# Seven products for the scores of the first two key tiles of a chunk, and three orders in a two-batch conformer block on one core

## The chip, the core and the metric

The kernel runs on one core of a Trainium2 chip. The metric is the device time of one execution in microseconds. The core has a matrix engine (PE, with its weight loads PEld beside it), a vector engine (DVE), an activation engine (ACT), a slow general engine (POOL), and a queue (SP) that issues nearly all DMA transfers. Each engine runs its own instructions strictly in the order in which they were written, and waits on semaphores of the others.

## The reference

One conformer block on x of 2 batches by 4000 tokens by 512 features, in bfloat16. Feed-forward 1 has a hidden width of 2048; attention has a single head of width 512; a convolution module with a batch norm and a second feed-forward follow.

```python
h = _layernorm(x); h = _silu(h @ w_ff1_a) @ w_ff1_b
x1 = x + 0.5 * h
h = _layernorm(x1); q, k, v = h @ w_q, h @ w_k, h @ w_v
scores = jnp.einsum('btd,bsd->bts', q, k) * scale
attn = jnp.einsum('bts,bsd->btd', _softmax(scores), v) @ w_o
x2 = x1 + attn
...
h = _layernorm(x3); h = _silu(h @ w_ff2_a) @ w_ff2_b
return _layernorm(x3 + 0.5 * h)
```

## The kernel before

**Tiling.** The tokens of both batches are cut into NCK = 16 chunks, eight to a batch: seven of 512 tokens and one of 416. The first feed-forward runs over all chunks, then attention over the query chunks g = 0 to 15 with 32 steps kt (one per 128 keys) in each, then the end of the convolution, then the second feed-forward over all chunks. The convolution of chunk g - 2 and the layer norm of chunk g - 1 run inside the attention steps of chunk g.

**Products.** Nearly all large products use a form of Strassen's method with seven products for a 2 by 2 block instead of eight. `score_quad` (L2096) does so for the scores of four key tiles at a time. Its left factors are parts of the transposed keys `hT` and three sums of them (`KF`, made by `k_sums`, L2069, once per batch and stored to DRAM as `kfd`, then loaded again for each later chunk by `k_stream`, L2091). Its right factors are parts of the transposed queries `qT` and four differences of them (`QF`). Four of its steps are spread over four values of kt, in PSUM banks 0 (c), 1 (x) and 2 (h). A step of the quad is: a few matmuls into a bank, then a copy by ACT or an addition by DVE, in PSUM, on which the next matmuls into that bank wait.

**The first two key tiles.** Of the 32 key tiles, 28 go into the seven quads (tiles 2 to 29). Tiles 0, 1 and 30 are computed plainly in `scores` (L1791): four matmuls of 512 columns each, into bank 0 for kt = 0 and bank 1 for kt = 1, and `exp_pair` (L1901) takes the exponential. At the same steps, `query_quad` (L1849) makes the transposed queries of the next chunk, in the same banks 0, 1 and 2: step 0 at kt = 31, steps 1 and 2 at kt = 0, step 3 at kt = 1.

**What else PE has at the start of a chunk.** `late_first`, `late_second` and `late_third` (L2229 to L2257) finish the product of probabilities and values of the chunk before, at kt = 0 to 6, in other banks; `conv_quad` (L2553) runs at kt = 2 to 7. The values of the new chunk begin at kt = 7.

**What sets the order.** The program text gives an order only within a tick. All operations are first collected in `Plan` (L112), with an assumed duration for each. A list schedule is made from these when the kernel is built: for PE among the operations within 8 us of PE time of the first one still open (`front` gives the products of a score quad 1 us of priority), for the other engines and the DMA queue among what is ready, the most urgent first. The emitted order on each engine is that of the plan; at run time nothing is reordered. An operation given to `either` may go to ACT or DVE, as the plan finds it better. `after(n, f)` puts f into the program n ticks later.

**The head.** `head` (L1237) makes the layer norm of the first four token tiles with `ln_tiles` (L1206, lag 1): on DVE the statistics (`ln_stats`), the mean and variance (`ln_mean`), then on POOL the power -0.5 (`ln_factor`), then the normalised tile on DVE, PE transposes, and blocks of the first product. `wa_sums` (L1409) makes four sums of the weights on DVE for the quads of chunk 1.

**The second feed-forward's second chunk.** Its layer norm is an `ln_job` (L1170) with all four tiles' statistics first, one POOL power for all, one `ln_shift`, four normalisations on ACT (`eng="ACT"`), and four DMA transposes on the SP queue. Its input tiles 2 and 3 are finished by `pw2_residual` only in chunk 0's steps f (their products stand at f = 2 and f = 4 of sixteen). `ff_weights` (L1321) makes sums of the second weight matrix on DVE, at the steps in `second.plan`.

Every recorded operation has the line L95 in the profile, that of the call object that issues it; groups are told apart by the names of the tiles.

Of the kernel before, what the change touches and what calls it, by code (L numbers as in the profile page):

```python
# [5 lines left out]
F32 = mybir.dt.float32  # L6
# [9 lines left out]
TILE = 128  # L16
# [543 lines left out]
class Conformer:  # L560
# [35 lines left out]
    def memory(self):  # L596
# [120 lines left out]
        self.hq = A.view(2048, QUADS * 2048).rearrange("p (q u r e j k) -> p q u r e j k", q=QUADS, u=2, r=2, e=2, j=2)  # L717
        self.kfd = nc.dram_tensor("kfd", [B, QUADS, 128, 1536], BF16, kind="Internal").ap()
        self.b_kfd = [[Buf("kfd") for _ in range(QUADS)] for _ in range(B)]
        self.vhd = nc.dram_tensor("vhd", [PAIRS, 128, 2 * D], BF16, kind="Internal").ap()  # L720
# [69 lines left out]
        self.thl = [W.view(24576 + s * 1024, CHUNK) for s in range(4)]  # L790
        self.b_thl = [W.buf("thl", 24576 + s * 1024, 2 * CHUNK) for s in range(4)]
        self.b_th = [W.buf("th", 24576 + s * 2048, 4 * CHUNK) for s in range(2)]
        homes = ((24576, 26624), (8192, 10240))
# [376 lines left out]
    def ln_job(self, c, kind, eng="DVE", plan=(1, 1, 2, 2, 3, 4, 5, 5, 6, 6), slot=None, pe=None):  # L1170
# [32 lines left out]
        for ti in range(n):  # L1203
            self.after(norm[ti], lambda ti=ti: tile(ti))

    def ln_tiles(self, c, sl, prepare=None, engs=("ACT", "ACT", "ACT", "DVE"), src=None, lag=2):  # L1206

# [11 lines left out]
        for ti in range(TPC):  # L1219
            if prepare:  # L1220
                prepare(ti)
            if ti and lag > 1:
                self.ln_mean(sl, ti - 1)
            self.ln_stats(c, sl, ti, src)
            if ti and lag > 1:
                self.ln_factor(sl, ti - 1)
            if ti >= lag:
                finish(ti - lag)
                yield ti - lag
            if lag == 1 or ti == TPC - 1:  # L1230
                self.ln_mean(sl, ti)
                self.ln_factor(sl, ti)
# [175 lines left out]

    def wa_sums(self, w, b_w, n, part):  # L1409

# [8 lines left out]
        for h in range(2):  # L1419
            self.S.op("DVE", lambda e, h=h: e.tensor_tensor(out=out[:, h], in0=x[:, h], in1=y[:, h], op=op),  # L1420
                      reads=more + rd, writes=wr)

# [646 lines left out]
    def k_sums(self, g, q, step):  # L2069

        S, n, b = self.S, (QUADS * g + q) % 2, g // TCB
        x = self.hq[:, q]
        b_x = [self.b_hT[kt // TPC][kt % TPC] for kt in self.quad_tiles(q)]
        if step == 4:
            self.store(self.kfd[b][q], self.KF[n].rearrange("p m u j k -> p (m u j k)"), self.b_KF[n], [self.b_kfd[b][q]])
            return
        a11, a12, a21, a22 = [x[:, :, r, e].rearrange("p u j k -> p u (j k)") for r in range(2) for e in range(2)]
        s1, s2, s4 = [self.KF[n][:, m].rearrange("p u j k -> p u (j k)") for m in range(3)]
# [3 lines left out]
        S.op("DVE", lambda e: e.tensor_tensor(out=out, in0=u, in1=v, op=op), reads=rd + b_x, writes=wr)  # L2082

    def k_here(self, g, q, half):
# [6 lines left out]
    def k_stream(self, g, q):  # L2091
        n, b = (QUADS * g + q) % 2, g // TCB
        self.load(self.KF[n].rearrange("p m u j k -> p (m u j k)"), self.kfd[b][q], self.b_KF[n],
                  reads=[self.b_kfd[b][q]])

    def score_quad(self, g, q, step):  # L2096
# [5 lines left out]
        b_t = [self.b_hT[kt // TPC][kt % TPC] for kt in self.quad_tiles(q)]  # L2102
        n = (QUADS * g + q) % 2
        part = lambda r, e: (lambda u, j: tiles[:, u, r, e, j], lambda u: b_t[2 * u + r])
# [97 lines left out]
    def forms(self, g, kt):  # L2202
# [637 lines left out]
    def program(self, any_score):  # L2840
# [50 lines left out]
        def ff1(c):  # L2891
            def hook(f):
# [261 lines left out]
        def ff2(c):  # L3154
            def hook(f):
# [106 lines left out]
```

## Time and profile before

| what | value |
|---|---|
| device time, median of 3 runs | 1855.84 us (1855.61 to 1857.74) |
| device time of the profiled execution | 1854.86 us |
| span of the profiled execution, first to last instruction | 1850.7 us |
| attention, one middle chunk (from one start to the next) | 61.6 us |
| DMA traffic | 228.51 MB, 123 GB/s on average |

The span is cut into the stages by the names of the tiles: the first feed-forward up to about 385 us, attention to about 1370 us, the end of the convolution to about 1403 us, the second feed-forward after that. Names on the left of an arrow are written, those on the right are read; `s` and `y` are PSUM banks 0 to 3 and 4 to 7, `sums`, `xt`, `keys`, `work` and `wff` are regions of SBUF that hold many things. A matmul's mean duration counts its way through the array, which overlaps the next one: the step from the start of one to the start of the next is what counts. Some matmul records are missing: a group of "x3" or "x7" with a gap of one matmul ahead of it had four or eight.

### The profile page before, as it was taken

To read this page: it belongs to the slowest core of one execution; us is meant where nothing else is said; L and a number is where in the kernel's file an instruction comes from. 1 tells how busy PE (TensorE), PEld (TensorE's weight loads), DVE (VectorE), ACT (ScalarE), POOL (GpSimd) and SP (SyncE) were. 2 spreads that over 40 slices of the span, in tenths; PEclk is the share of its full clock that TensorE was granted. 3 is DMA by queue.
4 is the path that set the end of the run, shared out by engine and by line. 5 is a ranking of instruction groups with operands and counts; after the bars stand their busy time and mean duration, and the time that the engine had idled before them with its cause. 6 is when DMAs were issued, how large, how long until landed. Compare 5 with 4: busy or idle time off the path is not lost.

```text
span 1850.7 us, 40576 instructions
## 1 busy us (share of the span) xinstructions
PE 1827.9 (99%) x15992; PEld 1512.7 (82%) x16090; DVE 1477.2 (80%) x3200; ACT 1358.0 (73%) x2412; POOL 145.8 (8%) x356
## 2 busy tenths in 40 slices
PE   9999999999999999999999999999999999999998
PEld 6888888866888888888778888888875888888887
DVE  8889998868766777677876777777778988888896
ACT  6887777755656877678776876787768778778776
POOL 3000000000000000000000000000010000000000
PEclk9999999999999999999999999999999999999999
DMA  8233344287645655457944434443466222221211
GB/s 202 84 91 85 83 113 98 70 240 231 183 130 142 180 161 152 119 142 175 244 136 130 129 108 115 137 125 104 125 213 171 56 70 72 66 58 48 61 35 56
DMA packets 312521, 228.51 MB, mean 123 GB/s; under 512 B 191154, under 2 KB 283125, under 8 KB 312068
## 3 DMA queue, kind: packets, MB, share of 16 engines
q1 hardware_dynamic: 311796, 225.59, 44.3%
q8 instruction: 128, 2.10, 0.5%
q14 instruction: 69, 0.57, 0.1%
q10 hardware_dynamic: 528, 0.26, 0.0%
HBM read 128.99 MB, written 55.82 MB: 100 GB/s over the span
## 4 chain that ended last, share of the span: by engine, by line
PE 92%; DVE 3%; DMA 2%; ACT 1%; issue 1%; SPq 0%; POOL 0%; DVEq 0%; ACTq 0%
PE y L95 48%; PE s L95 44%; DVE work L95 1%; DMA work<-work 1%; DVE sums L95 1%; ACT work L95 1%; DVE wff L95 0%; DVE xt L95 0%; DMA dcvd<-wff 0%; DVE s L95 0%; DVE keys L95 0%; ACT sums L95 0%; ACT keys L95 0%; DMA work<-lrowd 0%; DMA xt<-in_x_dram 0%
## 5 line engine op out<-in xcount | busy, mean ns | idle before, releaser
L95 ACT ACTIVATE sums<-s 128x512 bf16<-128x512 f32 (+4 forms) x498 | 291.4, 586 | 134.4 <-PE s L95 131.1
L95 ACT ACTIVATE keys<-s 128x512 bf16<-128x512 f32 (+3 forms) x275 | 157.1, 575 | 134.2 <-PE s L95 110.4
L95 DVE TENSOR_TENSOR sums<-sums 128x512 bf16<-128x512 bf16 (+3 forms) x528 | 202.1, 399 | 64.5 <-ACT sums L95 52.7
L95 PE MATMUL y<-work,keys 128*128 128x256 bf16 x1920 | 244.4, 273 | 0.6 <-DVE work L95 0.6
L95 PE MATMUL s<-sums 128*128 128x256 bf16 (+1 forms) x1428 | 212.5, 272 | 0.6 <-DVE s L95 0.3
L95 PE MATMUL y<-wff,keys 128*128 128x256 bf16 (+2 forms) x1590 | 208.9, 276 | 0.2
L95 ACT ACTIVATE work<-xt,work 128x512 bf16<-128x512 bf16 x264 | 202.6, 786 | 7.4 <-DVE work L95 5.6
L95 PEld LDWEIGHTS y<-work,keys 128*128 128x128 bf16 x1920 | 187.6, 98 | 23.6 <-DVE work L95 1.2
L95 PE MATMUL y<-sums,keys 128*128 128x256 bf16 (+1 forms) x1440 | 206.5, 270 | 0.0
L95 PE MATMUL s<-work,keys 128*128 128x256 bf16 (+4 forms) x1370 | 197.0, 282 | 2.3 <-DVE xt L95 0.6
L95 PE MATMUL y<-work,wff 128*128 128x256 bf16 (+3 forms) x1324 | 197.3, 272 | 1.0 <-ACT keys L95 0.8
L95 DVE TENSOR_TENSOR keys<-keys 128x1024 bf16<-128x1024 bf16 (+2 forms) x262 | 170.5, 665 | 22.3 <-ACT keys L95 17.9
L95 PEld LDWEIGHTS y<-wff,keys 128*128 128x128 bf16 (+1 forms) x1592 | 151.2, 98 | 30.2 <-issue 3.3
L95 DVE BATCH_NORM_STATS2 work<-xt 128x6 f32<-128x512 bf16 x251 | 163.2, 682 | 2.4 <-DMA xt<-in_x_dram 1.7
L95 PEld LDWEIGHTS s<-sums 128*128 128x128 bf16 x1428 | 138.9, 98 | 23.2 <-DVE s L95 0.6
L95 PEld LDWEIGHTS y<-sums,keys 128*128 128x128 bf16 x1440 | 138.1, 98 | 21.6 <-issue 3.3
L95 POOL TENSOR_TENSOR work<-work 128x4 f32<-128x4 f32 (+3 forms) x107 | 91.6, 858 | 766.7 <-DVE work L95 754.3
L95 PEld LDWEIGHTS s<-work,keys 128*128 128x128 bf16 (+1 forms) x1400 | 113.1, 97 | 43.4 <-ACT sums L95 2.2
L95 PEld LDWEIGHTS y<-work,wff 128*128 128x128 bf16 x1324 | 127.3, 98 | 18.8 <-issue 1.5
L95 PE MATMUL y<-sums,xt 128*128 128x256 bf16 (+1 forms) x960 | 140.9, 270 | 0.3 <-DVE sums L95 0.3
L95 PE MATMUL s<-xt,keys 128*128 128x256 bf16 (+1 forms) x872 | 132.6, 270 | 1.9 <-DVE s L95 1.6
L95 DVE TENSOR_TENSOR s<-s,xt 128x512 f32<-128x512 f32 (+1 forms) x119 | 81.5, 685 | 63.0 <-PE s L95 53.3
(162 smaller groups left out, 3345.1 us busy)
## 6 DMA issues: line engine op xcount, KB each, us to landing
xt<-kfd SPq DMA_DIRECT2D x98, 384.0 KB, 3.2
xt<-v12d SPq DMA_DIRECT2D x105, 256.0 KB, 3.1
xd<-xt SPq DMA_DIRECT2D x28, 512.0 KB
xt<-xd SPq DMA_DIRECT2D x28, 512.0 KB, 4.0
out_dram<-xt SPq DMA_DIRECT2D x14, 512.0 KB, 2.9
xt<-in_x_dram SPq DMA_DIRECT2D x13, 512.0 KB, 4.3
dcvd<-wff SPq DMA_DIRECT2D x48, 128.0 KB
keys<-dcvd SPq DMA_DIRECT2D x12, 512.0 KB, 3.9
```

The costliest lines, as they stand in the source:

```text
L95: return getattr(eng, self.name)(*self.args, **self.kw)
```

## The change

The scores of key tiles 0 and 1 are computed together by seven products of a half quad, `half_quad`, in the 13 chunks 2 to 7 and 9 to 15. Chunks 0, 1 and 8 keep the plain form. The sums of keys for it (`KF[0]`, half a quad's size) are made in chunks 1 and 8, stored, and loaded for chunks 3 to 7 and 10 to 15; the two homes of `KF` are numbered anew, so that in chunks other than 0 and 8 quad 0's sums lie in home 1; quad 0's load moves from kt = 25 to kt = 29 and quad 1's from kt = 29 to kt = 1 of its own chunk.

In the head, the statistics of a tile come after the mean of the tile before, and the first of `wa_sums` after the fourth normalised tile. The layer norm of the second feed-forward's chunk 1 is made in two halves (`ln_halves`), its normalisations on either engine. One `ff_weights` moves from f = 15 to f = 13.

```diff
+    def ln_halves(self, c, plan):
+        S, sl, s = self.S, self.nxt("ln", self.LN_SLOTS), c % 2
+        def factors(two):
+            for ti in range(two.start, two.stop):
+                self.ln_mean(sl, ti)
+            S.op("POOL", lambda e: e.tensor_tensor(out=self.rs[sl][:, two], in0=self.mv[sl][:, two, 1],
+                                                   in1=self.neghalf[0:TILE, two], op=ALU.pow),
...
+        def tile(ti):
+            self.ln_norm(c, sl, ti, self.ltm[ti][0:TILE, :], self.b_ltm[ti], "any")
+            self.transpose(self.lnT[s][:, ti], self.ltm[ti], [self.b_ltm[ti]], [self.b_lnT[s][ti]])
+        for k, at in enumerate(plan):
+            two = slice(2 * k, 2 * k + 2)
+            for n in range(2):
+                self.after(at[n], lambda ti=2 * k + n: self.ln_stats(c, sl, ti))
+            self.after(at[2], lambda two=two: factors(two))
+            self.after(at[3], lambda two=two: shift(two))
+            for n in range(2):
+                self.after(at[4 + n], lambda ti=2 * k + n: tile(ti))
...
-            self.ln_stats(c, sl, ti, src)
+            self.ln_stats(c, sl, ti, src, [self.b_mv[sl][ti - 1]] if ti and lag == 1 else ())
...
+    @staticmethod
+    def k_home(g, q):
+        return (q + (g % TCB > 0)) % 2 if q >= 0 else 0
...
+    def half_quad(self, g, step):
+        S, s, hw = self.S, g % TCB % 2, width(g) // 2
+        (cx, b_cx), (hy, b_hy) = self.bank(0), self.bank(2)
+        c, x = cx[:, 0:hw], cx[:, hw:2 * hw]
+        h, y = hy[:, 0:hw], hy[:, hw:2 * hw]
+        m5, b_m5 = self.m5h[:, 0:hw], self.b_m5h
...
+        def product(k, out, b_ps, start=False):
+            (a, b_a), (m, b_m) = forms[k]
+            for j in range(2):
+                self.mm(out, a(j), m(j), start and j == 0, j == 1, [b_a, b_m(j)], b_ps, skip_group_check=True)
+        def plus(out, b_out):
+            S.op("DVE", lambda e: e.tensor_tensor(out=out, in0=h, in1=m5, op=ALU.add), reads=[b_hy, b_m5], writes=[b_out])
+        if step == 0:
+            product(1, c, b_cx, True)
+            product(5, x, b_cx)
+            self.act(m5, x, AF.Copy, [b_cx], [b_m5])
+        elif step == 1:
+            self.act(h, c, AF.Copy, [b_cx], [b_hy])
+            product(6, h, b_hy)
+            product(2, c, b_cx)
+            plus(x, b_cx)
+        elif step == 2:
+            product(7, h, b_hy)
+            plus(y, b_hy)
+            product(3, x, b_cx)
+            self.exp_pair(g, 0, cx, b_cx)
+        else:
+            product(4, h, b_hy)
+            self.exp_pair(g, 1, hy, b_hy)
...
-                if plain and kt < KT - 1 or kt < 2 or kt == KT - 2:
+                if plain and kt < KT - 1 or g % TCB < 1 + (g < TCB) and kt < 2 or kt == KT - 2:
...
                     S.front(1000)
-                    self.score_quad(g, *divmod(kt - 2, 4))
+                    for step in ((0,), (1, 2), (3,))[kt] if kt < 3 and g % TCB > (g < TCB) else ():
+                        self.half_quad(g, step)
+                    if kt > 1:
+                        self.score_quad(g, *divmod(kt - 2, 4))
                     S.front(0)
...
+        for at in {1: (26, 27), TCB: (29, 30)}.get(g, ()):
+            if kt == at:
+                self.k_here(g, -1, kt % 2 == g % TCB)
...
-        if r == 0 and 1 < q and (g % TCB if q < QUADS else g and (g + 1) % TCB):
-            self.k_stream(g + q // QUADS, q % QUADS)
-        if g == 0 and kt == 30 or g == 1 and kt == 1:
-            self.k_stream(1, kt % 2)
+        if r == 0 and q and (g % TCB if q < QUADS else g and (g + 1) % TCB) and (q != QUADS or g % TCB > (g < TCB)):
+            self.k_stream(*((g, q) if q < QUADS else (g + 1, q - QUADS - 1)))
+        if g == 0 and kt == 30:
+            self.k_stream(1, 0)
...
-        second.plan = {(0, 12): (0,), (0, 15): (1,), (1, 0): (2,), (1, 8): (3,)}
+        second.plan = {(0, 12): (0,), (0, 13): (1,), (1, 0): (2,), (1, 8): (3,)}
...
-                    self.wa_sums(self.Wa, self.b_Wa, (0, 1, 3, 2)[f % 4], (f - 8) // 4)
+                    self.wa_sums(self.Wa, self.b_Wa, (0, 1, 3, 2)[f % 4], (f - 8) // 4, self.b_ltm[3:] if f == 8 else ())
...
-                        self.ln_job(1, "in", "ACT", (3, 4, 5, 7, 7, 8, 8, 8, 9, 9))
+                        self.ln_halves(1, ((2, 2, 3, 4, 5, 5), (5, 6, 7, 8, 8, 9)))
```

In the half quad, banks 0 and 2 hold two halves each: c and x (tile 0 for the two halves of the queries) in bank 0, h and y (tile 1) in bank 2. Every copy and addition in a bank excludes matmuls into the other half of that bank, since the bank is one buffer to the synchronisation.

More of the change, by code (lines that the diff above doesn't have):

```diff
@@ L717, in memory @@
         self.hq = A.view(2048, QUADS * 2048).rearrange("p (q u r e j k) -> p q u r e j k", q=QUADS, u=2, r=2, e=2, j=2)
-        self.kfd = nc.dram_tensor("kfd", [B, QUADS, 128, 1536], BF16, kind="Internal").ap()
-        self.b_kfd = [[Buf("kfd") for _ in range(QUADS)] for _ in range(B)]
+        self.hh = A.view(0, 1024).rearrange("p (r e n) -> p r e n", r=2, e=2)
+        self.kfd = nc.dram_tensor("kfd", [B, QUADS + 1, 128, 1536], BF16, kind="Internal").ap()
+        self.b_kfd = [[Buf("kfd") for _ in range(QUADS + 1)] for _ in range(B)]
         self.vhd = nc.dram_tensor("vhd", [PAIRS, 128, 2 * D], BF16, kind="Internal").ap()
@@ L1407, in ff_second, with wa_sums @@
                 f == 0, f == FC - 1, [self.b_Wb[f], b_p], b_ps, inc=inc)
-    def wa_sums(self, w, b_w, n, part):
+    def wa_sums(self, w, b_w, n, part, behind=()):
         at = slice(part * HF // 2, (part + 1) * HF // 2)
@@ L1420, in wa_sums @@
             self.S.op("DVE", lambda e, h=h: e.tensor_tensor(out=out[:, h], in0=x[:, h], in1=y[:, h], op=op),
-                      reads=more + rd, writes=wr)
+                      reads=more + rd + list(behind), writes=wr)
     def wa_ahead(self, w, step):
@@ L2082, in k_sums, with k_move @@
         S.op("DVE", lambda e: e.tensor_tensor(out=out, in0=u, in1=v, op=op), reads=rd + b_x, writes=wr)
+    @staticmethod
+    def k_home(g, q):
+        return (q + (g % TCB > 0)) % 2 if q >= 0 else 0
+    def k_move(self, g, q, away):
+        n, b = self.k_home(g, q), g // TCB
+        here, there = self.KF[n].rearrange("p m u j k -> p m (u j k)"), self.kfd[b][q % (QUADS + 1)].rearrange("p (m x) -> p m x", m=3)
+        if q < 0:
+            here, there = here[:, :, 0:HD], there[:, :, 0:HD]
+        if away:
+            self.store(there, here, self.b_KF[n], [self.b_kfd[b][q]])
+        else:
+            self.load(here, there, self.b_KF[n], reads=[self.b_kfd[b][q]])
     def k_here(self, g, q, half):
@@ L2102, in score_quad @@
         b_t = [self.b_hT[kt // TPC][kt % TPC] for kt in self.quad_tiles(q)]
-        n = (QUADS * g + q) % 2
+        n = self.k_home(g, q)
         part = lambda r, e: (lambda u, j: tiles[:, u, r, e, j], lambda u: b_t[2 * u + r])
```

33 lines of the change are left out of this document (24 added, 9 removed).

## The prediction

> **What bounds the kernel now.** I read the page first, then the busy time by windows, then the timeline of single engines at the three places that the change touches.
>
> ```profile
> span 1850.7 us, 40576 instructions
> PE 1827.9 (99%) x15992; PEld 1512.7 (82%) x16090; DVE 1477.2 (80%) x3200; ACT 1358.0 (73%) x2412; POOL 145.8 (8%) x356
> ...
> PE 92%; DVE 3%; DMA 2%; ACT 1%; issue 1%; SPq 0%; POOL 0%; DVEq 0%; ACTq 0%
> ```
>
> PE is busy for 1827.9 of 1850.7 us and is 92% of the chain that ends last. So a matmul taken away is worth its step in the stream, unless a wait takes the place; and only 22.8 us of PE's time are idle at all. The windows say where.
>
> ```profile
> 0.00:25.00 25.00, 22.25 (x167) 12.60 (x168) 20.87 (x63) 13.97 (x25) 5.70 (x17) 1.00 1.03 257
> ...
> 633.38:695.00 61.62, 61.40 (x548) 51.37 (x551) 47.05 (x109) 46.50 (x86) 4.14 (x16) 1.00 0.53 158
> ...
> 1400.00:1425.00 25.00, 21.85 (x155) 13.97 (x156) 21.18 (x47) 23.24 (x40) 2.41 (x3) 1.00 0.71 199
> 1425.00:1450.00 25.00, 24.44 (x205) 20.00 (x207) 23.25 (x42) 20.31 (x34) 1.01 (x1) 1.00 0.21 55
> 1450.00:1475.00 25.00, 24.36 (x209) 20.32 (x210) 22.44 (x46) 16.69 (x28) 1.01 (x1) 1.00 0.22 59
> ```
>
> The columns are the window, its length, then PE, PEld, DVE, ACT and POOL busy. A middle chunk of attention has 0.2 us of idle PE in 61.6, while DVE (47) and ACT (46.5) have room. The head has 2.75 us of idle PE, and the first 75 us of the second feed-forward 3.15 + 0.56 + 0.64 = 4.35 us. These are the change's three places: matmul time in attention, idle time at the other two.
>
> **The half quad: what it saves.** PE's timeline at the start of chunk 5 (start, duration, operation, count), and a piece of the chain of waits that is PE alone:
>
> ```profile
> 699.72 1.03 PE L95 MATMUL s<-work,keys 128*128 128x512 bf16 x4
> 700.58 0.60 PE L95 MATMUL s<-work,sums 128*128 128x256 bf16 x4
> ...
> 706.02 0.60 PE L95 MATMUL s<-xt 128*128 128x256 bf16 x4
> ...
> 715.19 0.60 PE L95 MATMUL s<-xt 128*128 128x256 bf16 x4
> ...
> 77.28 1.75 PE y L95 x16
> ```
>
> Four matmuls of 512 columns take 700.58 - 699.72 = 0.86 us, 0.215 each; sixteen of 256 take 1.75, 0.1094 each. Removed per chunk: 8 x 0.215 = 1.72 us. Added: 7 products of 2 matmuls, 14 x 0.1094 = 1.53. That saves 0.19 us in eleven chunks of 512 tokens, 2.1 us; in the two of 416 about 13/16 of it, 0.3 together. Sum **2.4 us**.
>
> [...]
>
> **What it adds elsewhere.** Per chunk two copies by ACT and two additions by DVE, 256 wide, in PSUM; no such width from PSUM stands in the trace, so I take the line through the two widths that do.
>
> ```profile
> L95 ACT ACTIVATE xt<-s 128x512 f32<-128x512 f32 x103 | 61.3, 595 | 33.0 <-PE s L95 32.3
> L95 ACT ACTIVATE xt<-s 128x416 f32<-128x416 f32 x16 | 8.2, 513 | 6.0 <-PE s L95 6.0
> L95 DVE TENSOR_TENSOR s<-s,xt 128x512 f32<-128x512 f32 x103 | 71.9, 698 | 52.2 <-PE s L95 46.8 <-ACT xt L95 4.0
> L95 DVE TENSOR_TENSOR s<-s,xt 128x416 f32<-128x416 f32 x16 | 9.6, 601 | 10.8 <-PE s L95 6.5 <-ACT xt L95 2.5 <-ACT work L95 1.6
> L95 DVE TENSOR_TENSOR sums<-sums 128x256 bf16<-128x256 bf16 x56 | 14.4, 278 | 11.9 <-ACT sums L95 11.7
> ```
>
> ACT: 595 - 256 x 82/96 = 0.38 us; DVE: 698 - 256 x 97/96 = 0.44. So 0.76 and 0.88 us a chunk on engines that are idle for 15 of 61.6. The key sums are four DVE operations of 0.28 us in chunks 1 and 8, also covered. If no cover were left, they would cost PE nothing directly, since PE waits only on the chain below.
>
> **The chain in bank 2.** This is what could take the saving back. After the change the half quad stands between the next chunk's query quad and quad 0, in the same banks, and its copy into bank 2 must wait for the query quad's last copy out of it.
>
> ```profile
> 701.27 1.08 ACT L95 ACTIVATE work<-s 128x512 bf16<-128x512 f32 x2
> ...
> 703.89 0.59 ACT L95 ACTIVATE s<-s 128x512 f32<-128x512 f32 x1
> ...
> 899.73 0.05 issue
> ```
>
> The two copies of the query quad end at 702.35; quad 0's copy of c into h starts at 703.89, and its product 6 at 706.02 (row above). The half quad's chain from 702.35: copy 0.43 (0.38, and 0.05 for each hand-over as in the last row), product 6 0.43 (one step and 0.27 to its end, which is what the 0.60 of four matmuls leaves after three steps, and the hand-over), addition 0.49, product 7 0.43, addition 0.49, product 4 0.43, exponential 0.65: 3.35 us, so 705.7. Quad 0's copy then ends at 706.3, and product 6 is late by 0.3 us against 706.02. Behind these instructions on PE stand, in program order, the products of late_third (60 matmuls, 6.6 us at 0.1094) and of the convolution, in other banks, and the plan may draw them ahead. I take the chain as covered, and 0 to 0.3 us of loss a chunk as its bounds: 2.4 - 3.9 = -1.5 at worst. Value: **2.3 us** saved.
>
> **The loads.** Eleven half-size loads and two stores are new, and quad 1's load now has to wait for the half quad's product 3.
>
> ```profile
> xt<-kfd SPq DMA_DIRECT2D x98, 384.0 KB, 3.2
> ...
> 710.85 0.32 SPq L95 DMA_DIRECT2D xt<-kfd  x1
> ```
>
> A load takes 0.32 us of the queue and lands 3.2 us after issue. If it goes out at about 706, behind product 3, it lands at 709.5; quad 1's product 5 stands at 715.19. What could be queued behind it on SP is the next load of quad sums, at 710.85. Cost 0, bounds 0 to 0.3 as above. Quad 0's load moves four steps nearer to its use and keeps five, 5 x 61.6/32 = 9.6 us.
>
> **The head.** DVE, POOL and PE in the first microseconds:
>
> ```profile
> 3.55 0.69 DVE L95 BATCH_NORM_STATS2 work<-xt 128x6 f32<-128x512 bf16 x1 [0.81 <-DMA xt<-in_x_dram]
> 4.69 0.69 DVE L95 BATCH_NORM_STATS2 work<-xt 128x6 f32<-128x512 bf16 x1 [0.45 <-DMA xt<-in_x_dram]
> 5.30 0.31 DVE L95 BATCH_NORM_AGGREGATE work<-work 128x2 f32<-128x9 f32 x2
> ...
> 9.08 0.89 DVE L95 TENSOR_TENSOR sums<-wff 128x512 bf16<-128x512 bf16 x2 [0.78 <-DMA wff<-in_w_ff_a_dram]
> 9.88 0.41 DVE L95 TENSOR_SCALAR work<-xt,work 128x512 bf16<-128x512 bf16 x1
> ...
> 8.09 0.62 POOL L95 TENSOR_TENSOR work<-work 128x1 f32<-128x1 f32 x1 [0.88 <-DVE work L95]
> ...
> 1.17 4.67 PE L95 MATMUL s<-work 128*128 128x512 bf16 x13 [1.17 <-DVE work L95]
> ...
> 6.75 0.88 PE L95 MATMUL y<-work 128*128 128x128 bf16 x8 [0.91 <-DVE work L95]
> ```
>
> Two in-order waits stand here. The second tile's statistics wait for their data at 4.69, and the first tile's mean, ready at 4.24, only runs behind them at 5.30: with the mean first, its power and normalised tile come some 0.8 us sooner, and PE's 0.91 us of waiting shrinks. Then `wa_sums` waits for its weights until 9.08 with the fourth normalised tile behind it, at 9.88, though POOL had its factor at 8.71: that tile moves by 1.1 us. What comes sooner here stays as long as DVE can follow. The bound is the idle time in the window less the 1.17 us before the first matmul, 2.75 - 1.17 = 1.6; below, 0, if DVE, busy for 20.87 of these 25 us, is late with something else (or -0.4, if another half of `wa_sums` takes the same place and waits likewise). Nearest to the fourth tile's row: **1.0 us**.
>
> **The second feed-forward's chunk 1.**
>
> ```profile
> 1402.00:1404.00 2.00, 0.89 (x10) 0.50 (x10) 1.93 (x5) 1.83 (x4) 0.70 (x1) 1.00 1.17 314
> 1404.00:1406.00 2.00, 1.48 (x16) 1.03 (x16) 1.97 (x7) 1.24 (x2) 0.00 (x0) 1.00 1.11 335
> ...
> 1403.44 0.69 DVE L95 BATCH_NORM_STATS2 work<-xt 128x6 f32<-128x512 bf16 x1
> 1412.27 0.70 DVE L95 BATCH_NORM_STATS2 work<-xt 128x6 f32<-128x512 bf16 x1
> ...
> 1415.23 2.92 ACT L95 ACTIVATE work<-xt,work 128x512 bf16<-128x512 bf16 x4
> ...
> 1416.06 5.14 SPq L95 DMA_TRANSPOSE work<-work  x4
> ...
> 1423.50 0.42 DVE L95 TENSOR_TENSOR sums<-work 128x512 bf16<-128x512 bf16 x1 [1.46 <-DMA work<-work]
> ...
> 1418.78 0.60 PE L95 MATMUL y<-work,wff 128*128 128x256 bf16 x4 [0.85 <-ACT keys L95]
> ```
>
> Tile 0's statistics are there at 1403.44, but all four normalisations wait for the last one's at 1412.27 and then fill ACT for 2.92 us; a copy that PE needs is queued behind them (0.85 us of PE at 1418.78), and DVE waits 1.46 us for the transposes, which take 5.14 us of the queue. In halves, two tiles and two transposes leave several us earlier, and the other two need only half of the 5.14 us of the queue ahead of DVE's sums. Normalisations may go to DVE (0.41 us in the head's row at 9.88) in place of ACT's 0.73. PE's idle time here is 4.35 us, of which 1.11 + 0.52 = 1.63 lie in the first two rows, ahead of anything that moves: at most 2.7 to gain; at least 0, if the early normalisations only push DVE's other work back. I take the wait of 0.85 and a small part of the rest: **1.1 us**. The moved `ff_weights` changes no amount of work: 0.
>
> **Sum.** 2.3 + 1.0 + 1.1 = 4.4 us off the profiled execution's 1854.86 (span 1850.7 and 4.16 around it): 1850.5. That execution lies 1.0 us below the median of the runs, 1855.84; against the median the sum gives **1851.4 us**, 0.24% faster.
>
> **Rivals.**
>
> *Only the matmuls pay (about 1853.5).* ACT and then DVE are at 23 of 25 us in the windows from 1400 to 1450; then the tiles that come sooner find DVE full, and the idle time moves and stays. The same in the head. Against it: at both places the rows name an in-order wait for something that is not yet there, not a full engine.
>
> *The chain in bank 2 decides (about 1863, slower).* The order on PE is fixed when the kernel is built, from assumed durations. If products 6, 7 and 4 of the half quad come to the head of PE's queue before their operand, PE stands still with ready work behind them. Three waits of 0.3 us are 0.9 us a chunk, 11.7 in thirteen: 4.4 - 11.7 is 7.3 us slower. It cancels the rest from 4.4/13 = 0.34 us a chunk. For it: two halves share a bank, so copies and additions also hold up products 2 and 3. [...] Against it: the same kind of chain runs seven times in each chunk now, with 0.2 us of idle PE in 61.6.
>
> *Weight loads no longer hide.* 14 loads of 98 ns replace 8; were they in the open, 256 columns would take 0.109 + 0.098 us, 14 of them 2.90 against 1.72, and 13 x 1.18 - 2.1 is 13 us slower, about 1869. [...]
>
> ```profile
> L95 PEld LDWEIGHTS s<-work,keys 128*128 128x128 bf16 x1144 | 109.5, 98 | 39.9 <-DVE xt L95 1.9 <-DVE sums L95 0.4 <-ACT sums L95 0.2
> ```
>
> *It doesn't show (about 1855.5).* The plan is made anew for the whole kernel; 22.8 us of idle PE lie in many places, and some of it may grow by as much as the edits bring.
>
> **How the numbers follow.** 0.2% of the median, 3.7 us, is about what a measurement of this kernel tells from no change. Forecast 0.60, its own range 1849.1 (all upper bounds, 2.4 + 1.6 + 2.7 = 6.7) to 1853, of which seven eighths lie beyond 3.7 us; only the matmuls 0.15; the chain 0.15, four fifths of it beyond the bound; no show 0.08; weight loads 0.02. Faster 0.55, the same 0.31, slower 0.14. The range 1849.0 to 1857.0 holds all but the slower cases.
>
> **What would show it.** In chunks 2 to 7 and 9 to 15 the plain score tiles fall from three to one, PE's busy time falls by about 0.19 us a chunk, and a chunk's length from 61.6 to 61.4. The fourth normalised tile starts near 8.8 us in place of 9.88, and the last blocks a microsecond sooner. The transposes of chunk 1 stand in two pairs, and the waits at 1418.78 and 1423.50 are gone or shorter. Wrong would be: waits of PE for ACT or DVE on `s` at every chunk's start, a load `xt<-kfd` that PE waits for, or idle PE after 1425 as long as before.

## The result and the profile after

The changed kernel takes 1852.26 us (median of 12 runs, 1850.49 to 1852.94), the kernel before in the same series 1855.45 (12 runs, 1852.80 to 1858.77): ratio 0.9979, 95% interval 0.9971 to 0.9987. A second series of the same instructions gave 0.9988 (0.9979 to 0.9997). So it is faster, by 0.1 to 0.2%, some 2 to 4 us. The profiled execution took 1851.06 us with a span of 1846.9, 3.8 less than before.

```profile
span 1846.9 us, 40836 instructions
PE 1827.6 (99%) x16082; PEld 1518.8 (82%) x16168; DVE 1491.3 (81%) x3240; ACT 1364.9 (74%) x2433; POOL 144.3 (8%) x357
PE 95%; DVE 2%; ACT 1%; DMA 1%; issue 1%; SPq 0%; DVEq 0%; ACTq 0%
```

The kernel is bound as before. PE's busy time seems to fall by 0.3 us only, where the matmuls should save 2.3. But some matmuls have no record (16168 weight loads stand beside 16082 matmuls, and 16090 beside 15992 before), and a missing one counts as idle. Two kernels of the experiments have all their records, one with the head's edits alone and one with the half quads alone:

```profile
PE 1833.5 (99%) x16090; PEld 1513.0 (82%) x16090; DVE 1476.3 (80%) x3201; ACT 1356.8 (73%) x2411; POOL 144.2 (8%) x356
```

```profile
PE 1830.7 (99%) x16168; PEld 1519.1 (82%) x16168; DVE 1490.1 (81%) x3234; ACT 1369.8 (74%) x2438; POOL 145.3 (8%) x356
```

Their difference is 2.8 us; with that of the second feed-forward's edits alone, also complete (1832.8), it is 2.1. But the other complete traces with half quads in all 13 chunks have 1830.7 to 1832.2, and busy time also counts the emptying of the array before a stall (0.16 us each, below). So it has the sign that was forecast, not the size; the size is read from a chunk's length.

The windows (length, then PE, PEld, DVE, ACT, POOL) tell where: three of the kernel after, then two of the kernel before, which are cut at the same matmuls as the first and the third:

```profile
664.40:725.82 61.42, 61.26 (x556) 51.84 (x557) 47.98 (x111) 47.51 (x88) 4.11 (x16) 1.00 0.61 169
1273.09:1336.58 63.49, 62.34 (x579) 53.22 (x582) 45.92 (x105) 48.18 (x93) 3.83 (x14) 1.00 0.43 126
1404.66:1459.77 55.11, 54.75 (x448) 43.95 (x454) 51.33 (x99) 45.84 (x78) 2.02 (x3) 1.00 0.34 89
```

```profile
664.23:725.83 61.60, 61.39 (x548) 51.35 (x551) 47.21 (x109) 46.57 (x86) 4.14 (x16) 1.00 0.55 164
1406.33:1464.45 58.12, 55.63 (x448) 43.67 (x454) 50.84 (x95) 48.56 (x82) 2.02 (x2) 1.00 0.34 95
```

An undisturbed chunk is 0.18 us shorter, as forecast. The stretch around the start of the last chunk has 1.15 us of idle PE in place of the usual 0.2, most of it one wait (below). The second feed-forward's first 55 us are 3.0 us shorter, with the same 448 matmuls.

**How much a stall costs.** In that last stretch the idle time fell by 2.13 us (58.12 - 55.63 less 55.11 - 54.75), the length by 3.01. These are the stalls of PE before, with the one at 1418.78 that the prediction shows:

```profile
1413.84 0.61 PE L95 MATMUL s<-sums 128*128 128x256 bf16 x4 [0.34 <-DVE s L95]
1431.50 1.05 PE L95 MATMUL y<-work,keys 128*128 128x256 bf16 x8 [0.33 <-DVE work L95]
1453.26 0.61 PE L95 MATMUL s<-sums 128*128 128x256 bf16 x4 [0.23 <-DVE sums L95]
1459.86 1.05 PE L95 MATMUL y<-work,keys 128*128 128x256 bf16 x8 [0.31 <-DVE work L95]
```

The five idle times add to 2.06 us. But the idle time begins only when the last matmul has left the array, 0.27 us after its start, where the next would have started after 0.109. So each stall costs its idle time and 0.16 us more: 2.06 + 5 x 0.16 = 2.9. That is near the 3.0 measured. In the kernel after all five are gone. Below, "lost" is this whole: the step between two starts less the first matmul's own step.

**Inside a half quad.** The kernel after, at the start of chunk 5, rows of ACT, PE and DVE in order of time:

```profile
702.31 0.37 ACT L95 ACTIVATE s<-s 128x256 f32<-128x256 f32 x1
702.73 0.39 PE L95 MATMUL s<-xt 128*128 128x256 bf16 x2
703.45 0.43 DVE L95 TENSOR_TENSOR s<-s,wff 128x256 f32<-128x256 f32 x1
704.49 0.38 PE L95 MATMUL s<-xt,keys 128*128 128x256 bf16 x2
704.90 0.43 DVE L95 TENSOR_TENSOR s<-s,wff 128x256 f32<-128x256 f32 x1 [0.43 <-PE s L95]
705.79 0.38 PE L95 MATMUL s<-xt,keys 128*128 128x256 bf16 x2
...
706.84 0.58 ACT L95 ACTIVATE s<-s 128x512 f32<-128x512 f32 x1
...
707.54 0.60 PE L95 MATMUL s<-xt 128*128 128x256 bf16 x4
```

The copy takes 0.37 us and an addition 0.43 (0.38 and 0.44 forecast). Quad 0's copy, 703.89 before, is 3 us later, but PE has other products all the while. So the chain fits, as long as DVE comes to the additions in time.

### The profile page after: what moved, and what is told of

It reads as the page before. It is cut to its first block, busy times and chain, and to the rows that moved or that the text cites. A ratio compares the mean times of both kernels' runs of the same rounds, so it can differ in the third digit from the quotient of the medians.

```text
span 1846.9 us, 40836 instructions
## 1 busy us (share of the span) xinstructions
PE 1827.6 (99%) x16082; PEld 1518.8 (82%) x16168; DVE 1491.3 (81%) x3240; ACT 1364.9 (74%) x2433; POOL 144.3 (8%) x357
## 4 chain that ended last, share of the span: by engine, by line
PE 95%; DVE 2%; ACT 1%; DMA 1%; issue 1%; SPq 0%; DVEq 0%; ACTq 0%
PE y L95 50%; PE s L95 45%; DVE work L95 1%; ACT work L95 0%; DVE wff L95 0%; ACT sums L95 0%; DMA work<-work 0%; DMA pqd<-wff 0%; ACT keys L95 0%; DVE xt L95 0%; DVE sums L95 0%; DVE s L95 0%; DMA xt<-kfd 0%; DVE keys L95 0%; ACT xt L95 0%
## 5 line engine op out<-in xcount | busy, mean ns | idle before, releaser
L95 PE MATMUL y<-sums,keys 128*128 128x256 bf16 (+1 forms) x1440 | 210.6, 270 | 0.0
L95 PE MATMUL s<-work,keys 128*128 128x256 bf16 (+4 forms) x1329 | 184.6, 275 | 1.0
L95 PE MATMUL s<-xt,keys 128*128 128x256 bf16 (+1 forms) x924 | 142.3, 270 | 1.2 <-DVE s L95 1.1
L95 PEld LDWEIGHTS s<-work,keys 128*128 128x128 bf16 (+1 forms) x1348 | 107.7, 97 | 34.9 <-ACT sums L95 2.2
L95 PE MATMUL s<-xt 128*128 128x256 bf16 (+1 forms) x893 | 131.4, 270 | 1.3 <-DMA xt<-kfd 0.9
```

The source lines that it names most:

```text
L95: return getattr(eng, self.name)(*self.args, **self.kw)
```

## The experiments

All kernels are timed in 11 or 12 runs beside the kernel before. An interval is about 0.09% to each side, 1.7 us, as large as most of the effects; so places are read from the trace of one execution of each. A ratio is to the kernel before in the same series; its median there was between 1854.15 and 1855.45 us, so medians of different series differ by up to 1.3 us for one and the same kernel. The table cuts each trace at three groups of matmuls found in all of them: the `s<-sums,keys` that waits 0.47 us near 925, the `s<-work` that waits some 0.35 us near 1369, and the end.

| kernel | to 925 | 925 to 1369 | to the end | median | ratio to before (95%) |
|---|---|---|---|---|---|
| before | 926.4 | 443.7 | 480.6 | 1855.45 | |
| changed | 924.4 | 444.1 | 478.5 | 1852.26 | 0.9979 (0.9971-0.9987) |
| changed, again | 923.9 | 444.1 | 479.0 | 1852.62 | 0.9988 (0.9979-0.9997) |
| half quads only | 923.8 | 446.4 | 478.8 | 1855.42 | 1.0003 (0.9994-1.0012) |
| head only | 925.0 | 443.6 | 480.6 | 1854.52 | 1.0002 (0.9992-1.0011) |
| second FF only | 926.1 | 443.9 | 479.6 | 1854.29 | 0.9998 (0.9989-1.0007) |
| no half quads | 925.0 | 444.1 | 478.9 | 1853.17 | 0.9989 (0.9980-0.9998) |
| earlier tail | 923.8 | 443.9 | 478.4 | 1851.70 | 0.9984 (0.9975-0.9993) |
| head mended | 924.3 | 444.5 | 479.0 | 1852.27 | 0.9990 (0.9981-0.9999) |
| halves on ACT | 924.1 | 444.2 | 479.9 | 1853.43 | 0.9989 (0.9980-0.9998) |
| transposes planned longer | 925.7 | 445.3 | 478.2 | 1852.66 | 0.9988 (0.9979-0.9997) |
| transposes more urgent | 924.3 | 442.9 | 481.2 | 1852.45 | 0.9986 (0.9977-0.9994) |
| first batch only | 924.2 | 444.2 | 479.2 | 1851.98 | 0.9984 (0.9976-0.9993) |
| tail and head | 923.5 | 443.7 | 478.6 | 1850.82 | 0.9978 (0.9969-0.9987) |

**Half quads only.** The other edits undone:

```diff
-            self.ln_stats(c, sl, ti, src, [self.b_mv[sl][ti - 1]] if ti and lag == 1 else ())
+            self.ln_stats(c, sl, ti, src)
-                    self.wa_sums(..., self.b_ltm[3:] if f == 8 else ())
+                    self.wa_sums(...)
-                        self.ln_halves(1, ((2, 2, 3, 4, 5, 5), (5, 6, 7, 8, 8, 9)))
+                        self.ln_job(1, "in", "ACT", (3, 4, 5, 7, 7, 8, 8, 8, 9, 9))
-        second.plan = {(0, 12): (0,), (0, 13): (1,), (1, 0): (2,), (1, 8): (3,)}
+        second.plan = {(0, 12): (0,), (0, 15): (1,), (1, 0): (2,), (1, 8): (3,)}
```

> Only the half quads are new; the head, the layer norm of the second feed-forward's chunk 1 and its weight sums are as before. Theory (matmul steps pay and the chain is covered): a middle chunk 0.18 us shorter, 2.3 us in all, less about 1.1 us where PE waits for quad 0's load of key sums in the last chunk (0.9 us before 1309 in the profile of the change, and the refilling of PE), so 1 to 2.5 us faster than the kernel before, with waits of 0.34, 0.85, 0.33, 0.23 and 0.31 us of PE still there between 1406 and 1460 us. Rival (the gain in the profile of the change was a new order of the plan that moved idle time): chunks still 0.18 us shorter but no wait for the load in the last chunk, or a total that doesn't follow the chunks. Rival (the chain in bank 2 decides): waits of PE for ACT or DVE on s at the start of each chunk, 0.3 us or more each.

No gain in the medians, and 1.7 us in the span, the size of a wait that was reordered far away (at 899, below). PE waits for DVE's additions at the starts of chunks 11 to 14, 0.93, 0.85, 1.00 and 0.54 us lost, and for the load in the last chunk, 1.12. The chain of waits at 1067 shows how, its last piece being PE's next product of the half quad:

```profile
1060.56 3.90 DMA work<-work
...
1064.59 1.37 DVE work L95 x3
1065.95 0.02 issue
1065.98 0.44 DVE work L95
...
1066.78 0.44 DVE s L95
1067.21 0.05 issue
1067.26 0.61 PE s L95 x4
```

A transpose lands 3.90 us after its issue; DVE stands on sums that need it, and behind these, in order, stands the half quad's addition. So the rival of the chain is a real one, but its price is set by a transfer and not by copies and additions: in kernels with half quads in the second batch, the last transpose ahead of each of these four chunk starts lands after 2.4 to 4.3 us.

**Head only** and **second feed-forward only**: the kernel before with those edits alone, as in the diff of the change.

> Only the order in the head is new. Theory: the statistics' order brings the first normalised tile sooner by about 0.3 to 0.5 us against the landing of its data, and the fourth tile stays near 9.7 us because another half of the weight sums waits in its place; 0.2 to 0.6 us faster, too little for the medians to tell. Rival (the prediction's 1.0 us): the fourth tile near 8.8 us and PE's work of the second chunk 1 us sooner.

> Only the halved layer norm of the second feed-forward's chunk 1 and the earlier weight sums are new. Theory: the five waits of PE between 1406 and 1460 us, 2.06 us idle, go, and each of them also cost some 0.16 us in which the array emptied and filled, so 2.9 us; 2.5 to 3.2 us faster. Rival (the prediction's bound: only idle time counts, 2.7 at most, 1.1 likely): 1 to 2.1 us faster, with some waits left. Rival (the half quads' new order of the plan took them away): the waits stay.

The head brings 0.4 us by the end of the first feed-forward: the 3400th weight load starts at 382.42 in place of 382.81. In the table it gains 1.4 us to 925, but 0.7 us are lost between 470 and 890, and 1.7 us are gained at 899. The kernel before has there, on DVE,

```profile
898.94 0.18 DVE L95 RECIPROCAL work<-work 128x4 f32<-128x4 f32 x1 [3.17 <-DMA work<-lrowd]
899.03 0.69 DVE L95 TENSOR_TENSOR s<-s,xt 128x512 f32<-128x512 f32 x1
```

and PE loses 1.71 us behind that addition. Here and in the changed kernel the plan has put the addition ahead of the reciprocal, with no edit near it; with the second feed-forward's edits alone it has not (1.53 lost). In that kernel four of the five stalls of 1406 to 1460 are gone, and 0.65 us at the other is left of 2.86 lost; a new one of 0.89 near 1697 takes part of it back, so 1.0 us net by the table.

Cut at the same weight loads, the stretch lasts 57.9 us before, 54.9 in the changed kernel, 55.7 with the second feed-forward's edits alone, and 56.1 with the half quads alone: there, with no edit near it, three of the five stalls are gone too. So of the 3.0 us at this place 1.2 to 2.3 belong to the edits, and the rest to the plan made anew.

**The load of key sums.** The scores of the last, short key tile of chunk 14 go eight steps earlier:

```diff
-                if kt == (21 if g == 0 else 24 if g < NCK - 1 else 16):
+                if kt == (21 if g == 0 else 24 if g < NCK - 2 else 16):
                     self.tail_scores(g)
```

> The changed kernel with the scores of the last, short key tile of chunk 14 eight steps earlier, so that the queue's wait for their way through DRAM no longer stands ahead of the load of quad 0's key sums for chunk 15. Theory (that load, late behind the queue's wait, costs 0.94 us of idle PE and the emptying of the array): PE's wait near 1309 us is gone and the kernel is 1.0 to 1.4 us faster than the changed kernel, about 1851. Rival (the home of the sums comes free too late, so the load is late anyway): the load still issues less than 3.2 us ahead of its product, and nothing is gained.

In the changed kernel the SP queue and PE in the last chunk look like this:

```profile
1299.09 0.42 SPq L95 DMA_DIRECT2D pqd<-wff  x1
...
1304.17 1.75 SPq L95 DMA_DIRECT2D wff<-pqd  x4
1306.02 0.42 SPq L95 DMA_DIRECT2D xt<-kfd  x1
...
1308.14 0.34 PE L95 MATMUL s<-work,xt 128*128 128x208 bf16 x2
1309.42 0.53 PE L95 MATMUL s<-xt 128*128 128x208 bf16 x4 [0.94 <-DMA xt<-kfd]
```

The tail's 32 KB go to DRAM and back. The queue stands from 1300.0 to 1304.17 for the landing of the way out, and quad 0's load, which the change moved from kt = 25 to kt = 29 and so past this wait, goes out at 1306.02 and lands 3.35 us later. With the tail earlier, the load goes out at 1302.53, its product stands at 1307.92 with no wait, and the kernel is 0.8 us shorter in span. The medians differ by 0.6 and 0.9, but are of other series, and the ratios (0.9984 against 0.9979 and 0.9988) tell no gain. The mechanism stands; the size is below the 1.0 to 1.4 us expected, and a new wait of 0.79 us near 1191 takes part of it.

**The changed kernel again**, unaltered:

> The changed kernel once more, nothing altered: a second execution of the same instructions in the trace, and its median beside those of this call. If the lost time at a place is set by the order of instructions it comes back with the same size (the load of key sums before 1309 us 1.10, the final layer norm's tile before 1611 us 1.09); if it hangs on when a transfer lands it moves (0.93 us before 553, 0.51 before 1129). Median 1851.5 to 1852.5 expected.

The load's wait (1.08 lost) and the layer norm's near 1611 (0.91) come back, as expected; so do those at 553 (0.69, from 0.93) and 1129 (0.56), which I had expected to move. The one at 553 is explained at the end.

**No half quads**: the changed kernel without them.

> The changed kernel without the half quads: the kernel before with the new head, the halved layer norm and the earlier weight sums. The single parts alone gave ratios of 1.0003 (half quads), 1.0002 (head) and 0.9998 (second feed-forward), and all together 0.9979. Theory (the parts add up; the half quads are worth about as much as the waits that they bring): 1850.5 to 1853 with chunks of 61.6 us, no wait of PE for DVE's additions on s at chunk starts, and none for the load of key sums in the last chunk. Rival (the half quads pay their 2.3 us): 1854 or above.

PE's waits for the additions and for the load are gone, as expected. Span 1848.1 against 1846.9 and 1847.0, median 1853.17 against 1852.62 in the same series, just between the two forecasts: within the changed kernel the half quads are worth about 1 us by the trace and not told from nothing by the medians. Nor is this the saving less the waits alone, since the kernel without them loses 0.49, 0.66 and 1.17 us near 673, 797 and 1161, where the changed kernel loses nothing. In the table they gain 0.7 to 1.1 us to 925 and nothing behind it, where the seven half quads should bring 1.2.

**Head mended.** All of the weight sums of the first half stand behind the fourth tile:

```diff
-                    self.wa_sums(self.Wa, self.b_Wa, (0, 1, 3, 2)[f % 4], (f - 8) // 4, self.b_ltm[3:] if f == 8 else ())
+                    self.wa_sums(self.Wa, self.b_Wa, (0, 1, 3, 2)[f % 4], (f - 8) // 4, self.b_lnT[0][3:] if f < 12 else ())
```

> The changed kernel with all of the weight sums of the first half behind the transposes of the fourth normalised tile, not the first sum alone. Theory (the in-order wait for the weights moved from one sum to the next): the fourth normalised tile starts right after its factor, near 9.0 us in place of 9.69, and the blocks on it come 0.5 to 0.7 us sooner; whether the end moves hangs on the first product of chunk 1, which needs these sums, so 0 to 0.7 us faster than the changed kernel. Rival: the fourth tile stays near 9.7, then POOL's factor or the statistics set it.

DVE in the changed kernel, then in this one:

```profile
9.35 0.43 DVE L95 TENSOR_TENSOR sums<-wff 128x512 bf16<-128x512 bf16 x1 [0.81 <-DMA wff<-in_w_ff_a_dram]
9.69 0.41 DVE L95 TENSOR_SCALAR work<-xt,work 128x512 bf16<-128x512 bf16 x1
```

```profile
8.76 0.41 DVE L95 TENSOR_SCALAR work<-xt,work 128x512 bf16<-128x512 bf16 x1 [0.51 <-POOL work L95]
```

In the changed kernel another sum took the freed place and waited likewise; with all of them behind, the tile waits for POOL alone. Against the kernel before, the 200th weight load starts 0.5 us sooner, and 0.2 to 0.3 in the two executions of the changed kernel. By the 3400th only 0.1 is left (0.3 in the changed kernel), since PE loses 0.44 us at a new wait near 61. So the mend works at its place, and this run doesn't show that the end moves; nor does the median.

**Halves on ACT.** The halved layer norm with its normalisations on ACT alone:

```diff
-            self.ln_norm(c, sl, ti, self.ltm[ti][0:TILE, :], self.b_ltm[ti], "any")
+            self.ln_norm(c, sl, ti, self.ltm[ti][0:TILE, :], self.b_ltm[ti], "ACT")
```

> The changed kernel with the normalisations of the halved layer norm on ACT alone, as before the change, in place of either engine. Theory (the halving itself, tiles and transposes that leave sooner, takes the waits of PE away between 1406 and 1460 us): the waits stay away, the stretch lasts 55.1 to 55.6 us and the median is that of the changed kernel, 1852.3 to 1852.6. Rival (moving normalisations off ACT does it): a wait of PE for ACT on keys near 1417 us comes back with 0.8 us or more, and others with it, so 1 to 3 us slower than the changed kernel.

The rival holds, with a span 1.3 to 1.4 us above the changed kernel's two. The changed kernel, then this one:

```profile
1407.01 0.73 DVE L95 TENSOR_SCALAR work<-xt,work 128x512 bf16<-128x512 bf16 x2
1407.45 2.52 SPq L95 DMA_TRANSPOSE work<-work  x2
...
1412.35 0.74 DVE L95 TENSOR_SCALAR work<-xt,work 128x512 bf16<-128x512 bf16 x2
1412.97 2.50 SPq L95 DMA_TRANSPOSE work<-work  x2
```

```profile
1413.49 2.92 ACT L95 ACTIVATE work<-xt,work 128x512 bf16<-128x512 bf16 x4
1414.32 5.15 SPq L95 DMA_TRANSPOSE work<-work  x4
1417.03 0.60 PE L95 MATMUL y<-work,wff 128*128 128x256 bf16 x4 [0.77 <-ACT keys L95]
```

Given either engine, the plan puts all four on DVE, at 0.37 us each and in two pairs. Bound to ACT, the halves fall together again into one row of 2.92 us, and three of the stalls are back (0.57, 0.93 and 0.59 lost). The stretch lasts 56.7 us, no shorter than the 56.1 with the half quads alone and the old layer norm: halving without another engine brings nothing here. Another engine without halving was not run, nor was the earlier `ff_weights` alone.

**Transposes in the plan.** Both with the earlier tail. One assumes 1.2 us more for a transpose's landing, the other makes it 2 us more urgent:

```diff
-                n.land = pipe - s + 1000 + behind
+                n.land = pipe - s + (2200 if n.turn else 1000) + behind
```

> The changed kernel with the last short tile's scores of chunk 14 earlier (as in the run before) and, in the plan, 1.2 us more assumed for the landing of a transpose (the traces have 3.3 us before 1064 where the plan has 2.1). Theory (the half quad's first addition stands on DVE behind sums that wait for transposes, and that wait is what costs PE 0.5 to 1.0 us a chunk in chunks 10 to 14): those waits of PE for DVE on s shrink below 0.3 us each; 0.5 to 2 us faster than the changed kernel, 1850 to 1851.5. Rival (DVE is late there for its load of work, not for the transposes): the waits stay as long.

```diff
-    ... - (self.SPARE if n.size else 0) ...
+    ... - (self.SPARE + 2000 * n.turn if n.size else 0) ...
```

> The changed kernel with the last short tile's scores of chunk 14 earlier, and the transposes 2 us more urgent in the plan (their assumed landing as it was). Theory (the half quad's first addition is late because DVE stands on sums whose transposes land late): with the transposes issued sooner DVE's waits for them ahead of the half quads go, and with them PE's waits of 0.5 to 0.8 us for DVE on s before 1129 and 1191 us; the stretch from 926 to 1351 us shortens by 1.0 us or more against the changed kernel's 425.6. Rival (DVE is late for its own load of work): these waits stay. In both the whole may move by 1 to 2 us either way at places far from the edit, as the plan is made anew; median 1850 to 1852.5.

In both, PE's waits for DVE at the starts of chunks 11 to 14 are gone, as the theory has it that ties them to the transposes. The urgent form shortens the stretch from 925 to 1369 to 442.9, 1.0 us below the earlier tail alone; up to 1350, where the forecast had its end, nothing is left of that (425.5 against 425.6), since three new waits of 0.72, 0.42 and 0.77 us stand behind 1343. Both lose elsewhere: the first waits 0.77 and 0.63 us near 45 and 1.46 and 0.93 near 1358, the second 0.84 near 1484. Neither is faster as a whole.

The 2.8 us that the second loses behind 1369 against the earlier tail are for the most part no matter of order. In the profiled execution the granted clock (the third figure from the end) was 0.50 for 3.4 us:

```profile
1402.40:1405.80 3.40, 3.40 (x21) 2.38 (x19) 3.09 (x9) 3.04 (x6) 0.70 (x1) 0.50 1.00 340
```

A matmul of 256 columns steps by 0.213 us there in place of 0.109, so half of the 3.4 us, 1.7, is lost (an estimate). No other trace has this before PE's last matmul, so the 481.2 of the table doesn't compare.

**Half quads in the first batch only**, with the earlier tail; the conditions on `g % TCB` become `1 < g < TCB`.

> The changed kernel with the last short tile's scores of chunk 14 earlier and half quads in chunks 2 to 7 only; chunks 9 to 15 compute key tiles 0 and 1 plainly. Theory (in the second batch the waits that the half quads bring, 1.4 to 1.7 us, take back the 7 x 0.18 = 1.2 us that they save): the stretch from 926 to 1351 us lasts 425.0 to 425.3 us, as in the kernels without half quads, against 425.4 to 425.7 with them; the median is that of the run with the earlier tail alone, 1851.7, within 0.5. Rival (the half quads pay there): the stretch is longer by about 1 us and the median 1852.5 or more.

Inconclusive. The median is the one expected, but the stretch to 1350 lasts 425.7 us, no shorter than with half quads: a wait of 1.21 us for DVE near 1099, in no other kernel, has taken the place of those removed. The changed kernel without any half quads has 425.6 there too, so the measure is too coarse for the question.

**Tail and head**: both mends, and nothing else.

> The changed kernel with both mends that showed at their own place: the last short tile's scores of chunk 14 earlier (PE's wait for the load of key sums in the last chunk gone, 1.1 us) and the weight sums of the first half behind the fourth tile's transposes (0.4 us by the end of the first feed-forward). Theory (places far apart add up where the plan between them stays alike): 1.0 to 1.5 us faster than the changed kernel, 1850.5 to 1851.5, its wait near 1309 us gone and the fourth normalised tile near 8.8 us. Rival (each edit makes the plan anew, and other waits of 0.5 to 1 us come and go with it): the two places show as said, but the median is that of the changed kernel, 1852 to 1853.

1850.82 us, ratio 0.9978 (0.9969 to 0.9987): the fastest median and span (1845.7) of all. Both places show as said: the fourth tile at 8.73, no wait for the load. The span is 1.2 and 1.3 us below the changed kernel's two, a gain of the size expected; by the ratios it is 0.2 and 1.9 us, so the timed runs don't tell it from nothing, nor from the earlier tail alone.

## Why the prediction was right, and where it was not

The forecast was 1851.4 us from a sum of 4.4, the result 1852.26 and 3.2 by the medians of that series. The total is near; the terms are not, and that their errors nearly cancel is luck: two terms were too large, one too small, and 1.7 us came from a place that the sum doesn't have.

*Half quads, 2.3 us.* The saving by matmul steps is right: 0.18 us in an undisturbed chunk against 0.19. Weight loads in the open, which one rival would have at 1.18 us a chunk, did not come. Net the half quads bring about 1. The step that failed is **the loads**, costed at 0 with 0.3 as its bound: it counted the queue's work behind quad 1's load, and kt distances for quad 0's, but not that quad 0's load was moved past the queue's wait for the tail's way through DRAM. It cost 1.10 us in one chunk, one of the signs of being wrong that the prediction names. **The chain in bank 2** was costed at 0 as well, and was covered in most chunks; the changed kernel lost 0.5 us at one start. The rival's three waits a chunk did not come, but its threshold of 0.34 us was passed where transposes land late, in four chunks of the half quads alone.

*The head, 1.0 us.* 0.3 to 0.4 by the end of the first feed-forward, with the head alone and in the changed kernel. The fourth tile moved by 0.2 in the changed kernel, whose first data landed 0.3 us later in the trace, and by 0.6 with the head alone, not by 1.1. The reason is the one given for the lower bound (another half of `wa_sums` takes the place); mended, it starts at 8.76, as forecast for the edit itself, but the runs don't show that this is kept. The other step, the first tile 0.8 us sooner, failed outright: the mean came 1.1 us sooner (5.30 before), the normalised tile not at all (6.33). The head alone:

```profile
4.23 0.20 DVE L95 BATCH_NORM_AGGREGATE work<-work 128x2 f32<-128x9 f32 x1
4.51 0.56 POOL L95 TENSOR_TENSOR work<-work 128x1 f32<-128x1 f32 x1 [3.01 <-DVE work L95]
...
5.72 0.69 DVE L95 BATCH_NORM_STATS2 work<-xt 128x6 f32<-128x512 bf16 x1
6.34 0.40 DVE L95 TENSOR_SCALAR work<-xt,work 128x512 bf16<-128x512 bf16 x1
```

The tile's power was there at 5.07, but DVE has the third tile's statistics ahead of the first normalised tile.

*The second feed-forward, 1.1 us.* 3.0 at the spot, beyond the bound of 2.7, of which 1.2 to 2.3 are due to the edits. The waits named went as forecast; the size was wrong twice. A stall costs 0.16 us more than its idle time, and not one stall but four went by the edits alone, five in the changed kernel. The cause named second, normalisations that may go to DVE, is the one without which the halving brings nothing. About 1 us of it is given back near 1611, where the remade plan has ACT wait for a final layer norm's factors (0.91 and 1.09 lost in the two executions).

*It doesn't show.* This rival's mechanism was at work beside the forecast: each edit reshuffled waits hundreds of microseconds away, by up to 1.7 us (at 899), as much as a term of the sum. So the parts don't add up: alone they shorten the span by 1.7, 1.6 and 1.1 us, together by 3.8, but 1.7 at 899 is in the first, the second and the whole, and the half quads alone lose 3.3 us at four chunk starts where the changed kernel loses 0.5. The ratios of 1.0003, 1.0002 and 0.9998 against 0.9979 add nothing to that, with intervals of 0.09% and 0.9988 for the same kernel in a second series. By stages, the changed kernel's 3.8 us are 2.0 before 925, of which 1.7 are that reordered wait, -0.4 in the stretch to 1369, and 2.1 behind it.

## What to carry to other kernels

Where an engine is 99% busy, count a stall as its idle time plus the time in which the pipe empties (0.16 us a stall here), and look for the few in-order waits behind a DMA before counting matmuls. When a load is moved, list every wait of its queue that it is moved past, the short way of other data through DRAM above all (1.10 us lost here). An edit that lets work go to the engine with room may do more than one that reorders it (the stretch lasts 54.9 us with it here, 56.7 without); and where the order is planned for the whole kernel, judge an edit at its own place and by several kernels, since distant waits move by as much as it brings (up to 1.7 us here).

## What was not expected of the hardware

A load ran late behind a fetch of instructions. In chunk 2, near 553, all ten traces with half quads there lose 0.5 to 1.1 us, the four without none, though SP, DVE and POOL have the same instructions in the same order there before and after. The kernel after, POOL and then PE, with DVE's addition between them queued behind what POOL releases:

```profile
551.62 0.11 POOL L95 MEMSET wff<- 128x2 bf16 x1 [1.41 <-DMA wff<-keysd]
...
553.12 0.61 PE L95 MATMUL s<-xt,keys 128*128 128x256 bf16 x4 [0.77 <-DVE s L95]
```

The 256 KB load `wff<-keysd`, issued at 546.88, lands after 4.69 us; before, after 3.06. The DMA queues in exactly these stretches, after and before:

```profile
q1 hardware_dynamic: 508, 1.03, 66.6%
q8 instruction: 1, 0.02, 1.7%
```

```profile
q1 hardware_dynamic: 416, 0.66, 67.9%
```

One packet of 16 KB on the queue of kind `instruction`, the fetch, stands in the first alone. In all ten traces with half quads such a packet starts 1.3 to 2.0 us after the load's issue and takes 0.9 to 1.3 us, and the load takes 4.2 to 4.8 us. In the four without, it starts 5.4 to 5.6 us after the issue, behind the landing, and the load takes 3.1 to 3.3.

The single packets show when. The load is 256 packets of 1 KB. In the kernel before the last of them starts 2.66 us after the issue. In the kernel after the fetch's packet lasts from 1.71 to 2.99 us; 240 packets have started by 2.90, and the other 16 run one behind the other from 2.98 to 4.18. From 2.99 to 3.72 the queue keeps 6.4% of the 16 DMA engines busy, where one of them makes 6.25%:

```profile
q1 hardware_dynamic: 6, 0.01, 6.4%
```

In all ten such a row of 16 packets begins within 0.05 us of the end of the fetch's packet. So a sixteenth of the load stood behind the fetch. That this is the share of the one DMA engine that carried the fetch is a reading of the 16 packets and the 6.4%; no view names a packet's engine. With the half quads DVE has 998 instructions ahead of the load's issue in place of 992 and PE 4678 weight loads in place of 4673, and the fetch comes some 4 us sooner against the load; that the one brings the other was not shown. The late load cost 0.8 us on average, of a change worth three.
